# Sorted-block attention with a feed-forward stage: the first score blocks, a Sinkhorn row and the order of three transfers are rearranged

## The chip, the cores and the metric

The kernel runs on one core of a Trainium2 chip. A core has a matrix engine (TensorE; PE in the profile, PEld its weight loads), VectorE (DVE), ScalarE (ACT), GpSimd (POOL) and SyncE (SP), which here only issues transfers. The engines run their own instruction streams in order and wait for each other on semaphores. SP and POOL issue DMAs on one queue each; 16 DMA engines carry them. The metric is device time in microseconds (us) of the whole program, lower is better. The time before is 219.33 us, the median of three runs (218.88 to 220.26).

## The reference

Four batches of 8 heads, 768 tokens, 64 values a head. A learned 8 x 8 matrix a head is made doubly stochastic by five Sinkhorn rounds and then mixes the blocks of 96 keys and of 96 values; the queries attend within their block, and the result goes through a feed-forward layer with squared ReLU.

```python
P = sort_net
for _ in range(5):
    P = np.exp(P - np.max(P, axis=-1, keepdims=True))
    P = P / (np.sum(P, axis=-1, keepdims=True) + 1e-09)
    P = P / (np.sum(P, axis=-2, keepdims=True) + 1e-09)
k_sorted = np.einsum('bhij,bhjcd->bhicd', P, k_b)
v_sorted = np.einsum('bhij,bhjcd->bhicd', P, v_b)
scores = scale * np.matmul(q_b, k_sb.transpose(0, 1, 2, 4, 3))
attn = np.exp(scores - np.max(scores, axis=-1, keepdims=True))
attn = attn / (np.sum(attn, axis=-1, keepdims=True) + 1e-09)
x = np.matmul(attn, v_sb)                 # then (B*S, H*D) = (3072, 512)
g = s * np.maximum(x @ w_in, 0.0) ** 2 + b
return g @ w_out                          # w_in 512 x 2048, w_out 2048 x 512
```

## The kernel before, in words

The order of every engine's instructions is the order in which the program is written; nothing is rescheduled. So what follows is also the order of the queues.

**Tiles.** Each batch is worked in two halves of four blocks (384 tokens). PSUM is shared by two pools: `psa`, three buffers of two banks (tag a), and `psb`, two buffers of one bank (tag b). A matmul group that takes a buffer waits until the one that had it before has been read out. Key, value and query tiles (`KS`, `VS`, `QT`) stand in SBUF.

**Start.** SP loads the Sinkhorn matrix and batch 0's values (L77, L81). GpSimd issues all other loads: queries of half 0 (`qh`, L106), keys (L95), then the weights `wi` and `wo`, in an order that is fixed from the start. VectorE and ScalarE run the Sinkhorn rounds on the tile `sn`, 32 rows of 8 x 8 (L241 to L263). L248 is the exponential on ScalarE; between the rounds ScalarE also casts batch 0's values into `VP` (L206). The 1e-9 is added in the first round only, by an instruction of its own (L261) from a tile `eps`. Meanwhile TensorE multiplies zeros (`warm`, L132): 16 products of 256 columns, 102 of 80 columns with 64 weights, 6 of 512.

**Front** (L594 to L623). `spread_first` spreads batch 0's rows of `sn` over the partitions by a matmul with `emat` (L270) into `pe`. `build_pd` makes from it the mixing matrix `PD` on VectorE: product with a selector (L286), sum over j (L289), sum over that (L291), reciprocal (L293), scaled product (L295). `q_banks` transposes the queries of half 0 on TensorE, 48 transposes into two `psb` buffers, which VectorE and ScalarE copy out. `spread_later` spreads the rows of batches 1 to 3 into `pel`, copied by ScalarE (L282). Then `k_piece` and `k_banks` make the mixed keys, 16 columns a piece (64 or 2 x 16 matmuls), `v_piece` the mixed values, `s_banks` and `s_piece` the scores of a head pair with the exponential on ScalarE, `p_piece` the product with the values (L486), its reciprocal (L491) and scaling into `x` (L492), `t_piece` the transposes of `x` for the feed-forward layer (L503), and `part` its first products (L537). `evac` copies a PSUM tile on the engine named: D for VectorE, A for ScalarE. `v_piece` with `halves` copies its two halves apart, the second one when the function that it returns is called.

**The rest.** `ffn1(t)` (L537) and `ffn2(t)` (L563) are the feed-forward layer for half t, and carry the attention work of later batches in slots: slot i of `ffn1` behind product pair i, slot i of `ffn2` behind four products. For batches 2 and 3 the dictionary `s1` of `halves` places score pieces `SC(n, half, pair)` (L441), output pieces `P` and the transposing DMA `TD` of a finished half (`t_dma`, L512) into the slots of `ffn2(2b + 1)`. Values of batches 2 and 3 are mixed in `v_tiles`, written to DRAM by four DMAs (`v_back`, L415) and read back in another layout by two (L419, one for each z), and the queries are transposed by two DMAs (`q_dma`, L520), all four on SP's queue, in that order, from slot 2 of `ffn1(2b)`. `store` sends the result (L588, L591). `make_bias` waits for the scalar b and for the weights `wo`; behind its copies GpSimd issues the last three query loads of batch 1.

Of the kernel before, what the change touches and what calls it, by code (L numbers as in the profile page):

```python
# [22 lines left out]
def kernel(  # L23
# [51 lines left out]

    sn = const.tile([BH, NB, NB], FP)
    nc.sync.dma_start(out=sn, in_=sort_net.rearrange("b h i j -> (b h) i j"))  # L77
# [50 lines left out]

    def warm(n, w=512, m=128):
        z = psb.tile([128, 512], FP, tag="b", name="z")  # L130
        for _ in range(n):
            nc.tensor.matmul(out=z[0:m, 0:w], lhsT=zeros[:, 0:m], rhs=zeros[:, 0:w],  # L132
                             start=True, stop=True)
# [52 lines left out]
    rrec = const.tile([BH, NB], FP)  # L186
    eps = const.tile([BH, NB], FP)
    nc.vector.memset(eps, 1e-9)
    jsel = const.tile([128, NB], FP)
# [27 lines left out]

    def q_banks(b, half, engs):
        if b not in QT:
            QT[b] = trp.tile([128, 2, NHP, CQ, 64], BF, tag="qt", name="qt")  # L220
        pr = slice(half * 64, (half + 1) * 64)
        for u in range(2):
            tr = psb.tile([128, 1024], BF, tag="b", name="tqb")
            for a in range(2 * u, 2 * u + 2):
                for c in range(CQ):
                    for e in range(2):
                        o = (a % 2 * CQ + c) * 64
                        nc.tensor.transpose(out=tr[e * 64:(e + 1) * 64, o:o + 64],  # L228
                                            in_=QH[b][pr, 2 * a + e, c, :],
                                            identity=ident[pr, pr])  # L230
            evac(engs[u], QT[b][:, half, 2 * u:2 * u + 2].rearrange("p a c t -> p (a c t)"),
                 tr[:, 0:2 * TG])

# [9 lines left out]
                            op=ALU.subtract)  # L243
    warm(16, 256)
    warm(102, 80, 64)
    warm(6)
    for it in range(5):
        nc.scalar.activation(out=sn, in_=sn, func=AF.Exp)  # L248
        for c in {1: (0,), 3: (1,), 4: (2, 3)}.get(it, ()):
            permute(nc.scalar, 0, v0f, slice(c * CV, (c + 1) * CV))  # L250
        if it in (1, 2):
            idle[it - 1]()
        nc.vector.tensor_reduce(out=rstat, in_=sn, axis=AX.X, op=ALU.add)
        nc.vector.reciprocal(out=rrec, in_=rstat)
        nc.vector.tensor_tensor(out=sn, in0=sn, in1=rrec.broadcast_to([BH, NB, NB]), op=ALU.mult)
        if it == 4:
            break
        nc.vector.tensor_reduce(out=rstat, in_=sn.rearrange("p i j -> p j i"),
                                axis=AX.X, op=ALU.add)
        if it == 0:  # L260
            nc.vector.tensor_tensor(out=rstat, in0=rstat, in1=eps, op=ALU.add)  # L261
        nc.vector.reciprocal(out=rrec, in_=rstat)
        nc.vector.tensor_tensor(out=sn, in0=sn, in1=spread(rrec, [[0, NB], list(rrec.ap[1])]),  # L263
                                op=ALU.mult)
# [8 lines left out]
    def spread_first():  # L273
        pe = psb.tile([128, 512], FP, tag="b", name="pe")
        spread_rows(0, pe[:, 0:NB * NB])
        return pe[:, 0:NB * NB]

    def spread_later():
        ps = psa.tile([128, 2, 512], FP, tag="a", name="pel")
        for b in range(1, B):  # L280
            spread_rows(b, ps[:, 0, (b - 1) * NB * NB:b * NB * NB])
        nc.scalar.copy(out=later.rearrange("p b n -> p (b n)"), in_=ps[:, 0, 0:(B - 1) * NB * NB])  # L282

    def build_pd(b, rows):
        tmp = rtp.tile([128, NB, NB], FP, tag="tmp", name="tmp")
        nc.vector.tensor_tensor(out=tmp, in0=rows.rearrange("p (i j) -> p i j", j=NB),  # L286
                                in1=spread(jsel, [[0, NB], list(jsel.ap[1])]), op=ALU.mult)
        pt = rtp.tile([128, NB], FP, tag="pt", name="pt")
# [62 lines left out]

    def v_piece(b, d0, eng, halves=None):
        ps = psa.tile([128, CK, 2 * NG], FP, tag="a", name="tv")
        for d in range(CK):
            for z in range(2):
                nc.tensor.matmul(out=ps[z * GAP:(z + 1) * GAP, d, :],  # L356
                                 lhsT=VP[b % 2][:, d0 + d, :], rhs=PD[b][:, :, z, :],
                                 start=True, stop=True)
        if halves is None:
            evac(eng, VS[b % 2][:, :, d0:d0 + CK], ps[0:KR].rearrange("p d g -> p g d"))  # L360
            return None

# [4 lines left out]

        half(0, eng)
        return lambda eng: half(1, eng)

# [40 lines left out]
    def v_back(b):  # L411
        w = 2 * NC * D
        vd = drp.tile([2 * 2 * NB, NHP, 4, w], BF, tag="vd", name="vd")
        for c in range(4):
            nc.sync.dma_start(out=vd[:, :, c],  # L415
                              in_=RAW["v", b][c * 32:(c + 1) * 32].rearrange(
                                  "p (a x) d -> p a (x d)", a=NHP))
        for z in range(2):
            nc.sync.dma_start(  # L419
                out=VS[b % 2][z * GAP:z * GAP + C2, :, 0:D],  # L420
                in_=vd[z * 2 * NB:(z + 1) * 2 * NB].rearrange("i a c (y d) -> (c y) (i a) d", d=D))

# [238 lines left out]
    def VT(b, r): return lambda: v_tiles(b, r)  # L661
    def VB(b): return lambda: v_back(b)
    def TD(b, h): return lambda: t_dma(b, h)
    def PDB(b): return lambda: build_pd(b, later[:, b - 1, :])
    def QD(b): return lambda: q_dma(b)
    def LV(b): return lambda: load("v", b, 6, QT[b - 1][:, NB - 1, 0, 0:1])


    def halves(n):
# [4 lines left out]
        else:  # L674
            s0 = {0: [KP(n, 0), KP(n, 1), KP(n, 2)]}
        s1 = {0: [SC(n, 0, 0), SC(n, 0, 1)], 2: [SC(n, 0, 2), SC(n, 0, 3), SC(n, 1, 0)],
              3: [P(n, 0, 0)], 4: [P(n, 0, 1)], 5: [P(n, 0, 2)],
              6: [P(n, 0, 3), TD(n, 0), P(n, 1, 0)], 8: [SC(n, 1, 1), SC(n, 1, 2), SC(n, 1, 3)],
              9: [P(n, 1, 1)], 10: [P(n, 1, 2)], 11: [P(n, 1, 3), TD(n, 1)]}
        if n == 1:  # L680
            s1[0] = [VP2(n, 3, "AD")] + s1[0]
            s1[3] = s1.pop(2)
            s1[4] = [P(n, 0, 0)]
            s1[5] = [P(n, 0, 1), P(n, 0, 2)]
        if n + 1 < B:
# [22 lines left out]
    for b in range(1, B):  # L708
        n = b + 1
        s0, s1, u0, v0 = {}, {}, {}, {}  # L710
        if n < B:
# [4 lines left out]
            v0 = {0: [VT(n, 0)], 2: [VT(n, 1)]}  # L716
            u0 = {2: [VB(n), QD(n)]}
            if n + 1 < B:
# [35 lines left out]
```

## Time and profile before

| what | value |
|---|---|
| median of three runs | 219.33 us (218.88 to 220.26) |
| the profiled execution | 219.04 us, its span 217.3 us |
| VectorE, ScalarE, GpSimd busy | 125.4, 114.7, 71.9 us |
| feed-forward products, L537 and L563 | 86.7 and 81.7 us busy |
| first real matmul (L270) | 11.39 us |
| last matmul ends, last store lands | about 214.4, 216.3 us |
| TensorE's clock over the span | 0.992 of full speed |

The page gives busy times, a strip of 40 slices, the chain of work that ended last and the costliest groups of instructions. The chain names at each step who released it. "Idle before" is the time an engine stood still just before an instruction, with what ended it. A window's row gives the busy time of each engine in that stretch and the clock that TensorE was granted. All durations come from this one profiled execution.

### The profile page before, as it was taken

Reading aid. Unit: us, or ns where it says so; the run is one execution under the profiler, and the core shown is the slowest. Engines: PE = TensorE matmul, PEld = TensorE weight load, DVE = VectorE, ACT = ScalarE, POOL = GpSimd, SP = SyncE. Lnnn points to the kernel's source line nnn. Section 1 sums busy time; section 2 is a strip of 40 time slices with the busy share of each in tenths; the row PEclk is TensorE's granted clock in tenths of the full one; section 3 lists DMA queues with packets and bytes.
Section 4 is the critical chain, followed back from the end, with each engine's and each line's share of the span. In section 5 each row is a group of like instructions: output and inputs, shape, how many; then the busy total and the mean of one; then the engine's idle time right before and its main releaser. Section 6 shows DMA issues by size and latency. Waiting matters only on the chain.

```text
span 217.3 us, 5268 instructions
## 1 busy us (share of the span) xinstructions
PE 209.4 (96%) x2197; PEld 123.8 (57%) x2216; DVE 125.4 (58%) x259; ACT 114.7 (53%) x162; POOL 71.9 (33%) x129
## 2 busy tenths in 40 slices
PE   7999999999999999999999899999999999999994
PEld 5887666655455555565445556654445566654454
DVE  6767456558886986447537675448318644442122
ACT  4678687648986436565533447655341456650000
POOL 7659782789906025910050027610000000000000
PEclk9979999999999999999999999999999999999999
DMA  5999999999939948999989587999991550001212
GB/s 160 275 169 126 123 161 206 205 188 143 130 71 241 195 110 160 190 143 110 113 205 188 126 146 143 182 129 79 78 242 51 121 124 0 0 0 49 99 48 97
DMA packets 68023, 28.92 MB, mean 133 GB/s; under 512 B 51872, under 2 KB 64288, under 8 KB 68000
## 3 DMA queue, kind: packets, MB, share of 16 engines
q0 software_dynamic: 31168, 12.85, 52.9%
q1 hardware_dynamic: 36832, 15.74, 38.7%
q8 instruction: 17, 0.28, 0.6%
q14 instruction: 6, 0.05, 0.1%
HBM read 28.85 MB, written 7.86 MB: 169 GB/s over the span
## 4 chain that ended last, share of the span: by engine, by line
PE 73%; DMA 15%; DVE 5%; SPq 4%; issue 2%; ACT 1%; POOL 0%
PE ops L563 30%; PE hps L537 30%; DMA qt<-qtok 5%; DMA xt<-x 5%; DMA vd<-rawv 4%; PE pv L486 3%; SPq L419 3%; PE sc L441 2%; PE ops L580 2%; PE tv L356 1%; DVE x L492 1%; PE tp L315 1%; DMA sn<-in_sort_net_dram 1%; PE tqb L228 1%; PE tpp L328 1%
## 5 line engine op out<-in xcount | busy, mean ns | idle before, releaser
L537 PE MATMUL hps<-xt,wi 128*128 128x384 bf16 x512 | 86.7, 326 | 0.7 <-DMA xt<-x 0.5
L563 PE MATMUL ops<-wo,gt 128*128 128x512 bf16 x350 | 81.7, 379 | 1.9 <-issue 1.1
L551 ACT ACTIVATE rt<-hps 128x768 bf16<-128x768 f32 x64 | 51.8, 811 | 30.6 <-PE hps L537 29.4
L537 PEld LDWEIGHTS <-wi 128*128 128x128 bf16 x512 | 48.7, 98 | 33.2 <-issue 1.5
L552 DVE TENSOR_TENSOR gt<-rt 128x768 bf16<-128x768 bf16 x64 | 36.4, 571 | 40.4 <-ACT rt L551 40.3
L563 PEld LDWEIGHTS <-gt 128*128 128x128 bf16 x368 | 33.9, 98 | 36.7
L588 DVE SCALAR_TENSOR_TENSOR ot<-ops,s_bc,bias 128x512 f32<-128x512 f32 (+2 forms) x27 | 18.5, 690 | 30.6 <-PE ops L563 28.1
L449 ACT ACTIVATE at<-sc 112x768 bf16<-112x768 f32 x24 | 17.8, 808 | 26.8 <-PE sc L441 26.7
L492 DVE TENSOR_TENSOR x<-pv,rec 96x512 bf16<-96x512 f32 x32 | 22.0, 687 | 1.1
L117 POOL DMA_DIRECT2D qtok<-in_q_dram x24 | 18.6, 797 | 3.2 <-issue 1.7
L486 PEld LDWEIGHTS <-at 112*128 112x128 bf16 (+1 forms) x256 | 12.3, 101 | 5.6 <-ACT vs L214 0.3
L214 ACT CAST ks<-tpp 64x512 bf16<-64x512 f32 x18 | 13.1, 725 | 4.5 <-DVE ks L216 4.1
L142 POOL DMA_DIRECT2D wi<-in_moe_w_in_dram x24 | 12.9, 572 | 5.0 <-DMA rawk<-in_k_dram 3.1
L216 DVE CAST ks<-tpp 64x512 bf16<-64x512 f32 x18 | 13.1, 727 | 0.9 <-ACT ks L214 0.6
L486 PE MATMUL pv<-vs,at 112*128 112x66 bf16 (+1 forms) x256 | 12.9, 195 | 0.2 <-ACT vs L214 0.2
L95 POOL DMA_DIRECT2D rawk<-in_k_dram x21 | 11.2, 546 | 2.8 <-issue 1.8
L95 POOL DMA_DIRECT2D rawv<-in_v_dram x18 | 9.7, 555 | 5.4 <-DMA wo<-in_moe_w_out_dram 4.0
L132 PE MATMUL z<-zeros 128*64 128x80 bf16 (+2 forms) x123 | 9.6, 253 | 1.3 <-DVE zeros L120 1.2
L491 DVE RECIPROCAL rec<-pv 96x8 f32<-96x8 f32 x32 | 6.3, 198 | 5.5 <-PE pv L486 5.3
L132 PEld LDWEIGHTS <-zeros 128*64 128x64 bf16 (+1 forms) x124 | 7.3, 130 | 3.0 <-DVE zeros L120 1.2
L90 POOL COPY rawv<-qt 128x1 bf16<-128x1 bf16 x2 | 0.4, 189 | 23.4 <-DMA qt<-qtok 23.4
L408 ACT CAST rawv<-tvs 128x384 bf16<-128x384 f32 x4 | 1.9, 478 | 9.1 <-PE tvs L403 5.1
(101 smaller groups left out, 142.8 us busy)
## 6 DMA issues: line engine op xcount, KB each, us to landing
out_dram<-ot SPq DMA_DIRECT2D x22, 256.0 KB, 2.9
rawv<-in_v_dram POOLq DMA_DIRECT2D x18, 128.0 KB, 5.6
rawk<-in_k_dram POOLq DMA_DIRECT2D x18, 128.0 KB, 4.4
qtok<-in_q_dram POOLq DMA_DIRECT2D x24, 96.0 KB, 6.5
wo<-in_moe_w_out_dram POOLq DMA_DIRECT2D x4, 512.0 KB, 10.3
v0f<-in_v_dram SPq DMA_DIRECT2D x4, 384.0 KB, 5.3
vd<-rawv SPq DMA_DIRECT2D x8, 192.0 KB, 4.9
vs<-vd SPq DMA_DIRECT2D x4, 384.0 KB, 12.9
```

The source lines that it names most:

```text
L95: nc.gpsimd.dma_start(out=ti[:, c:c + n, :].rearrange("p c d -> p (c d)"), in_=raw["qkv".index(t)][b][:, c * D:(c + n) * D])
L117: nc.gpsimd.dma_start(out=QTOK[b][:, n], in_=qv[:, n])
L132: nc.tensor.matmul(out=z[0:m, 0:w], lhsT=zeros[:, 0:m], rhs=zeros[:, 0:w], start=True, stop=True)
L214: nc.scalar.copy(out=out, in_=in_)
L449: nc.scalar.activation(out=at, in_=sc[0:KR, :, 0:TG], func=AF.Exp, scale=scale)
L486: nc.tensor.matmul(out=pv[0:m, e, n * VW:(n + 1) * VW], lhsT=atf[:, c0:c0 + m], rhs=VS[b % 2][:, e * NG + g(n), :], start=True, stop=True)
L492: nc.vector.tensor_tensor(out=x[:, :, hp * 128:(hp + 1) * 128].rearrange("p n (e d) -> p e n d", e=2), in0=pvv[:, :, :, 0:D], in1=rec.unsq ...
L537: nc.tensor.matmul(out=H1[t, i][:, f, 0:TG], lhsT=wi[:, hp, fc:fc + 128], rhs=XT[t][:, :, hp, :], start=(hp == 0), stop=(hp == NHP - 1))
L551: nc.scalar.activation(out=rt, in_=h, func=AF.Relu)
L552: nc.vector.tensor_tensor(out=gt[:, 2 * i:2 * i + 2, :], in0=rt, in1=rt, op=ALU.mult)
L563: nc.tensor.matmul(out=ops, lhsT=gt[:, f, m * 128:(m + 1) * 128], rhs=wo[:, f, :], start=(f == 0), stop=(f == NF - 1))
L588: nc.vector.scalar_tensor_tensor(out=ot[:, ns], in0=ops, scalar=s_bc, in1=BIAS[0][:, ns], op0=ALU.mult, op1=ALU.add)
```

## The change

It has five parts.

1. Sinkhorn: `sn` becomes the first 8 rows of a tile `sne` with a ninth row set to 1e-9. The first round's sum over columns runs over the nine rows; the addition of `eps` goes. 
2. The zero products before the front become 42 of 256 columns; 8 more wait for a small memset (`gate`) that VectorE does in the fourth round. Three of 512 columns stand behind `spread_later`, in its tile's second bank.
3. `build_pd` takes the sum `cs` as the accumulated output of its first product (all batches); the reduction L291 goes.
4. Front: the transposes of the queries stand ahead of the first spread, their copies behind `build_pd`. `pe` takes a `psa` buffer. `later` is copied by VectorE. The first value piece stands ahead of `k_banks`, which is copied by ScalarE alone; two more value pieces stand ahead of the scores. The halves of the last two value pieces are copied by VectorE first, then by ScalarE.
5. Batches 2 and 3: SP issues read z = 0, query transpose 0, read z = 1, query transpose 1. In `ffn2(2b + 1)` three score pieces stand in slot 0 instead of two, the first output piece in slot 2 instead of 3, and the others follow a slot earlier, with the transposing DMA of half 0 in slot 5 instead of 6.

```diff
-    sn = const.tile([BH, NB, NB], FP)
+    sne = const.tile([BH, NB + 1, NB], FP)
+    sn = sne[:, 0:NB, :]
...
+    gate = const.tile([128, 16], BF)
+
+    def warm(n, w=512, z=None, behind=None):
+        if z is None:
+            z = psb.tile([128, 512], FP, tag="b", name="z")
+        if behind is not None:
+            nc.tensor.matmul(out=z[:, 0:16], lhsT=zeros[:, 0:128], rhs=behind,
+                             start=True, stop=True)
...
-    eps = const.tile([BH, NB], FP)
-    nc.vector.memset(eps, 1e-9)
+    nc.vector.memset(sne[:, NB:NB + 1, :], 1e-9)
...
-    warm(16, 256)
-    warm(102, 80, 64)
-    warm(6)
+    warm(42, 256)
     for it in range(5):
...
+        if it == 3:
+            nc.vector.memset(gate, 0.0)
+            warm(8, 256, behind=gate)
...
-        nc.vector.tensor_reduce(out=rstat, in_=sn.rearrange("p i j -> p j i"),
+        nc.vector.tensor_reduce(out=rstat, in_=(sn if it else sne).rearrange("p i j -> p j i"),
                                 axis=AX.X, op=ALU.add)
-        if it == 0:
-            nc.vector.tensor_tensor(out=rstat, in0=rstat, in1=eps, op=ALU.add)
...
     def spread_later():
         ps = psa.tile([128, 2, 512], FP, tag="a", name="pel")
         for b in range(1, B):
             spread_rows(b, ps[:, 0, (b - 1) * NB * NB:b * NB * NB])
-        nc.scalar.copy(out=later.rearrange("p b n -> p (b n)"), in_=ps[:, 0, 0:(B - 1) * NB * NB])
+        warm(3, z=ps[:, 1])
+        nc.vector.tensor_copy(out=later.rearrange("p b n -> p (b n)"), in_=ps[:, 0, 0:(B - 1) * NB * NB])
...
-        nc.vector.tensor_tensor(out=tmp, in0=rows.rearrange("p (i j) -> p i j", j=NB),
-                                in1=spread(jsel, [[0, NB], list(jsel.ap[1])]), op=ALU.mult)
+        cs = rtp.tile([128, 1], FP, tag="cs", name="cs")
+        nc.vector.scalar_tensor_tensor(
+            out=tmp, in0=rows.rearrange("p (i j) -> p i j", j=NB), scalar=1.0,
+            in1=spread(jsel, [[0, NB], list(jsel.ap[1])]), op0=ALU.mult, op1=ALU.mult, accum_out=cs)
         pt = rtp.tile([128, NB], FP, tag="pt", name="pt")
         nc.vector.tensor_reduce(out=pt, in_=tmp, axis=AX.X, op=ALU.add)
-        cs = rtp.tile([128, 1], FP, tag="cs", name="cs")
-        nc.vector.tensor_reduce(out=cs, in_=pt, axis=AX.X, op=ALU.add)
...
-    def q_dma(b):
+    def q_dma(b, vd=None):
         ti = QTOK.pop(b)
         qt = trp.tile([128, NB, NHP, BLK], BF, tag="qt", name="qt")
         for n0 in (0, HB):
+            if vd is not None:
+                v_read(b, vd, n0 // HB)
             nc.sync.dma_start_transpose(
...
+    qe = q_banks(0, 0)
     build_pd(0, spread_first())
-    q_banks(0, 0, "DA")
+    qe("DA")
     spread_later()
     k_piece(0, 0, "D")
     k_piece(0, CK, "A")
-    k_banks(0, 2 * CK, "DA")
     v_piece(0, 0, "D")
+    k_banks(0, 2 * CK, "AA")
+    v_piece(0, CK, "D")
+    v2 = v_piece(0, 2 * CK)
     s_banks(0, 0, 0)
     s_piece(0, 0, 1)
-    v_piece(0, CK, "D")
-    v2 = v_piece(0, 2 * CK, "A", 1)
-    v3 = v_piece(0, 3 * CK, "A", 1)
-    v2("D")
+    v2(0, "D")
+    v3 = v_piece(0, 3 * CK)
+    v3(0, "D")
+    v2(1, "A")
+    v3(1, "A")
     s_banks(0, 0, 2)
-    p_piece(0, 0, 0, 3)
-    v3("A")
+    p_piece(0, 0, 0)
     p_piece(0, 0, 1)
...
-        s1 = {0: [SC(n, 0, 0), SC(n, 0, 1)], 2: [SC(n, 0, 2), SC(n, 0, 3), SC(n, 1, 0)],
-              3: [P(n, 0, 0)], 4: [P(n, 0, 1)], 5: [P(n, 0, 2)],
-              6: [P(n, 0, 3), TD(n, 0), P(n, 1, 0)], 8: [SC(n, 1, 1), SC(n, 1, 2), SC(n, 1, 3)],
+        s1 = {8: [SC(n, 1, 1), SC(n, 1, 2), SC(n, 1, 3)],
               9: [P(n, 1, 1)], 10: [P(n, 1, 2)], 11: [P(n, 1, 3), TD(n, 1)]}
...
+            s1.update({0: [SC(n, 0, 0), SC(n, 0, 1), SC(n, 0, 2)],
+                       2: [SC(n, 0, 3), P(n, 0, 0), SC(n, 1, 0)], 3: [P(n, 0, 1)],
+                       4: [P(n, 0, 2)], 5: [P(n, 0, 3), TD(n, 0)], 6: [P(n, 1, 0)]})
```

`v_read(b, vd, z)` is the read of L419 for one z. Batch 1 keeps its slots.

More of the change, by code (lines that the diff above doesn't have):

```diff
@@ L127 @@
     nc.scalar.activation(out=dummy, in_=zeros[:, 0:1], func=AF.Exp)
-    def warm(n, w=512, m=128):
-        z = psb.tile([128, 512], FP, tag="b", name="z")
+    gate = const.tile([128, 16], BF)
[5 more added lines that the diff above has]
+                             start=True, stop=True)
         for _ in range(n):
-            nc.tensor.matmul(out=z[0:m, 0:w], lhsT=zeros[:, 0:m], rhs=zeros[:, 0:w],
+            nc.tensor.matmul(out=z[:, 0:w], lhsT=zeros[:, 0:128], rhs=zeros[:, 0:w],
                              start=True, stop=True)
@@ L216, in evac, with q_banks @@
             nc.vector.tensor_copy(out=out, in_=in_)
-    def q_banks(b, half, engs):
+    def q_banks(b, half, engs=None):
         if b not in QT:
@@ L221, in q_banks @@
         pr = slice(half * 64, (half + 1) * 64)
+        trs = []
         for u in range(2):
             tr = psb.tile([128, 1024], BF, tag="b", name="tqb")
+            trs.append(tr)
             for a in range(2 * u, 2 * u + 2):
@@ L230, in q_banks, with move @@
                                             identity=ident[pr, pr])
-            evac(engs[u], QT[b][:, half, 2 * u:2 * u + 2].rearrange("p a c t -> p (a c t)"),
-                 tr[:, 0:2 * TG])
+        def move(engs):
+            for u in range(2):
+                evac(engs[u], QT[b][:, half, 2 * u:2 * u + 2].rearrange("p a c t -> p (a c t)"),
+                     trs[u][:, 0:2 * TG])
+        if engs is None:
+            return move
+        move(engs)
     idle = [
@@ L273, in spread_first @@
     def spread_first():
-        pe = psb.tile([128, 512], FP, tag="b", name="pe")
-        spread_rows(0, pe[:, 0:NB * NB])
-        return pe[:, 0:NB * NB]
+        pe = psa.tile([128, 2, 512], FP, tag="a", name="pe")
+        spread_rows(0, pe[:, 0, 0:NB * NB])
+        return pe[:, 0, 0:NB * NB]
     def spread_later():
@@ L350, in k_banks, with v_piece @@
             evac(eng, KS[b % 2][:, :, :, c1:c1 + CK // 2], ps.rearrange("p c z g -> p g z c"))
-    def v_piece(b, d0, eng, halves=None):
+    def v_piece(b, d0, eng=None):
         ps = psa.tile([128, CK, 2 * NG], FP, tag="a", name="tv")
@@ L358, in v_piece @@
                                  start=True, stop=True)
-        if halves is None:
+        if eng is not None:
             evac(eng, VS[b % 2][:, :, d0:d0 + CK], ps[0:KR].rearrange("p d g -> p g d"))
-            return None
         def half(h, eng):
@@ L366, in half @@
                  ps[0:KR].rearrange("p d (g i) -> p g i d", i=NB)[:, :, hs])
-        half(0, eng)
-        return lambda eng: half(1, eng)
+        return half
     def v_pairs(b, d0, engs):
@@ L417, in v_back, with v_read @@
                                   "p (a x) d -> p a (x d)", a=NHP))
[L418 to L421, printed above, removed]
+        return vd
+    def v_read(b, vd, z):
+        nc.sync.dma_start(
+            out=VS[b % 2][z * GAP:z * GAP + C2, :, 0:D],
+            in_=vd[z * 2 * NB:(z + 1) * 2 * NB].rearrange("i a c (y d) -> (c y) (i a) d",
+                                                          d=D))
     AT = {}
@@ L661, in VT, with QD @@
     def VT(b, r): return lambda: v_tiles(b, r)
-    def VB(b): return lambda: v_back(b)
     def TD(b, h): return lambda: t_dma(b, h)
     def PDB(b): return lambda: build_pd(b, later[:, b - 1, :])
-    def QD(b): return lambda: q_dma(b)
+    def QD(b): return lambda: q_dma(b, v_back(b))
     def LV(b): return lambda: load("v", b, 6, QT[b - 1][:, NB - 1, 0, 0:1])
@@ L675, in halves @@
             s0 = {0: [KP(n, 0), KP(n, 1), KP(n, 2)]}
-        s1 = {0: [SC(n, 0, 0), SC(n, 0, 1)], 2: [SC(n, 0, 2), SC(n, 0, 3), SC(n, 1, 0)],
-              3: [P(n, 0, 0)], 4: [P(n, 0, 1)], 5: [P(n, 0, 2)],
-              6: [P(n, 0, 3), TD(n, 0), P(n, 1, 0)], 8: [SC(n, 1, 1), SC(n, 1, 2), SC(n, 1, 3)],
+        s1 = {8: [SC(n, 1, 1), SC(n, 1, 2), SC(n, 1, 3)],
               9: [P(n, 1, 1)], 10: [P(n, 1, 2)], 11: [P(n, 1, 3), TD(n, 1)]}
         if n == 1:
[L681 to L684, printed above, removed]
+            s1.update({0: [VP2(n, 3, "AD"), SC(n, 0, 0), SC(n, 0, 1)],
+                       3: [SC(n, 0, 2), SC(n, 0, 3), SC(n, 1, 0)], 4: [P(n, 0, 0)],
+                       5: [P(n, 0, 1), P(n, 0, 2)], 6: [P(n, 0, 3), TD(n, 0), P(n, 1, 0)]})
+        else:
+            s1.update({0: [SC(n, 0, 0), SC(n, 0, 1), SC(n, 0, 2)],
+                       2: [SC(n, 0, 3), P(n, 0, 0), SC(n, 1, 0)], 3: [P(n, 0, 1)],
+                       4: [P(n, 0, 2)], 5: [P(n, 0, 3), TD(n, 0)], 6: [P(n, 1, 0)]})
         if n + 1 < B:
@@ L716 @@
             v0 = {0: [VT(n, 0)], 2: [VT(n, 1)]}
-            u0 = {2: [VB(n), QD(n)]}
+            u0 = {2: [QD(n)]}
             if n + 1 < B:
```

## The prediction

> **What bounds the kernel now.** First the page: how much is TensorE idle at all?
>
> ```profile
> PE 209.4 (96%) x2197; PEld 123.8 (57%) x2216; DVE 125.4 (58%) x259; ACT 114.7 (53%) x162; POOL 71.9 (33%) x129
> ...
> PEclk9979999999999999999999999999999999999999
> ```
>
> TensorE is busy 209.4 of 217.3 us, and the third slice has a granted clock of 0.7. So the kernel is bound by TensorE, and a change gains only by starting the real matmuls sooner, by removing holes, or by removing that dip. The profiled execution took 219.04 us (span 217.3, and 1.7 around it), 0.29 below the median 219.33; I add and subtract from 219.04. Next the chain of waits, in order of time (start, length, what):
>
> ```profile
> 11.03 0.23 DVE sn L255
> 11.25 0.14 issue
> 11.39 0.40 PE pe L270 x2
> 11.79 0.88 PE tqb L228 x48
> 12.67 0.81 PE pel L270 x6
> 13.48 1.82 PE tp L315 x64
> 15.30 0.85 PE tkb L346 x32
> 16.15 0.87 PE tv L356 x32
> 17.04 1.24 DVE vs L216
> ```
>
> Until 11.25 the chain is the Sinkhorn loop on VectorE (the busy TensorE there does filler products). From 11.39 it is TensorE in program order: 48 query transposes stand between the first spread and the key tiles. Then the granted clock, in four stretches of 3.41 us (start:end, length, then busy us and instructions of PE, PEld, DVE, ACT, POOL, then clock, DMA share, GB/s):
>
> ```profile
> 10.08:13.49 3.41, 2.87 (x64) 2.12 (x64) 2.29 (x10) 3.29 (x5) 0.88 (x2) 1.00 1.16 202
> 13.49:16.90 3.41, 3.41 (x128) 3.38 (x128) 1.98 (x3) 2.25 (x4) 2.85 (x6) 0.50 1.10 137
> 16.90:20.31 3.41, 3.16 (x127) 2.56 (x123) 2.99 (x3) 2.81 (x6) 3.41 (x7) 1.00 1.06 128
> 20.31:23.73 3.42, 3.07 (x54) 2.40 (x54) 2.86 (x9) 2.93 (x7) 2.73 (x6) 1.00 1.09 131
> ```
>
> The clock is halved for exactly one stretch, 13.49 to 16.90, right behind the stretch with the least work on PE. Last, PE's waits from 100 us on (who, for whom, us in total, times, longest):
>
> ```profile
> PE hps L537 <- DMA xt<-x: 0.5, 1, 0.5
> PE sc L441 <- DMA qt<-qtok: 0.2, 1, 0.2
> ```
>
> These two are the only waits on data there, at 124.5 (batch 2, first half's transposed output) and 158.9 (batch 3, query transposes). Everything else after 26 us is TensorE back to back.
>
> **The change, part by part.**
>
> *Sinkhorn.* The 1e-9 add (L261) goes: 0.19 us, from its start at 4.31 to the next at 4.50. The ninth row makes one reduction 72 elements long instead of 64; two reductions of 64 take 0.21 and 0.26, so at most 0.03 more. The memset of that row replaces the memset of `eps`; the `gate` memset (that of `eps` took 0.07) falls into VectorE's 0.32 us wait for Exp. If that cover were gone it would cost 0.07. `sn` is ready at 11.06 instead of 11.24, and the first spread starts at 11.20 instead of 11.39.
>
> *Query transposes first.* They wait for `qh`, which by the trace lands at 9.62, and take 0.8 to 0.9 us: 9.75 to 10.6, done 0.6 before the spread. Their cover is the Sinkhorn loop. If `qh` landed later than 10.3 they would hold up the spread one for one. Both fillers before them are over: 42 products of 256 columns at 0.213 (their spacing up to 6.6 us) and 0.109 behind that end near 8.4; the 8 behind `gate` run from about 8.45 to 9.4.
>
> *Behind the spread.* TensorE then has 6 spread products (0.13 apart, as at 12.60 to 13.21), 0.79, and three 512-column fillers at 0.216 (spacing of the fillers at 10.04 to 10.47), 0.65: 11.46 to 12.9. VectorE: tmp, pt, rc, pd at their old spacings 0.26, 0.25, 0.20, 0.35 from 11.64, the L291 sum (0.20) gone: pd ready at 12.70, plus 0.12 to reach PE. No row has a product with an accumulated sum; between the plain product tmp (0.22) and the larger L295 (0.35), plus a second instruction as long as the sum removed, pd comes at 12.70 to 13.0. I take 12.8; the fillers hide it. So `tp` starts at 12.9 instead of 13.41: 0.5 us.
> The Trainium skill ("VectorE: DVE Perf Modes", Two Vector instructions with no wait between them) says that an operation that writes out its accumulator is two instructions, the operation and an accumulator read. By it pd would come at the 13.0 end and the sum would be 0.1 smaller; no run here shows it yet.
>
> *Order of the tiles.* With the clock at full, a 32-product group takes 0.5 us (value tiles from 17.38) against 0.85 in the halved stretch. VectorE then evacuates without a hole: tp0 at 13.6, value tiles at 14.8 and 15.9 (starts 1.14 apart, as 17.04 and 18.19), two halves at 17.0 and 17.9. Before, its fourth value evacuation ended at 20.37; now at 18.6. VectorE got the copy of `later` (0.30) and lost a key evacuation (0.69); ScalarE got the second small key evacuation (0.59) and lost the copy. ScalarE: tp1 14.1 to 15.1, two `tkb` to 16.15, three Exps 16.6 to 18.25, two value halves to 19.3. `pv` of the first head pair needs `v2`'s buffer, freed at 18.8: it starts at 18.9 instead of 20.31. But ScalarE's Exps of the third score tile end at 20.1 (before: 21.02), the fourth's scores wait for them, and the last x ends at 23.0 instead of 24.22. The next transposes of queries start at 24.9 instead of 26.0: **1.0 us**, of which 0.7 is the dip that is not there (the same replay of the old order at full clock ends 0.7 earlier) and 0.35 the order itself.
>
> *Does the dip go?* The stretch ahead of it had 2.87 us of PE, 0.95 of it transposes, so 1.92 of other products. The new order puts into the same stretch two and six spreads (0.40 and 0.88 in busy time), the three fillers (about 0.8) and 0.5 of key tiles: about 2.5 without transposes. The stretch from 20.31 held full clock with 3.07, of which three groups of output transposes (0.33 each) are 1.0: 2.1 of others. 2.5 is above it, 1.92 below; so in the same alignment the dip goes. (With transposes counted, 2.87 lost the clock, 3.07 held it, and the new order has about 3.0: less clear.)
> The Trainium skill ("TensorE: Matmul & The Clock Gate", Part 1, and Part 4 on transposes) has a free-running window of 3413 ns and says that transposes do not count as busy in the same way. The length agrees with the trace (3.41); by a free-running window the alignment changes from run to run.
>
> *Batches 2 and 3.* `v_read` of half 0, transposes of query half 0, then `v_read` and transposes of half 1, instead of both reads first. On SP's queue the first transpose is moved past one read: before, SP issued the second read for 5.84 us and the transpose landed at 158.98; now one read less is ahead, and it lands some 6 us earlier. The 0.26 hole at 158.9 closes (0.2 and the semaphore). The third scores move to slot 0, the first output piece to slot 2, and the transposing DMA of half 0 to slot 5, one slot (4 products, 0.87) earlier; the wait at 124.5 (0.5) closes, since its landing at 124.86 moves by more than that. The stores queued behind it on SP have DMA landings of 2.9 us and no one on PE waits for them. Scores 0 to 2 fill all three `psa` buffers; the first Exp (0.81) frees one long before the 8 products (1.73) to slot 2 are over, so no new wait. Sum: **0.7**.
>
> Last, `make_bias`: VectorE waits for `b_bc` there anyway (1.6), and the query loads behind it set when batch 1's second transpose lands (65.8). Its scores start at 67.1, so at most 1.2 us of the front's gain gets past this point; 1.0 does. Total 219.04 - 1.0 - 0.7 = 217.3; with the accumulator's upper end 217.4.
>
> **Rivals.**
>
> *A: the clock drops all the same.* With the 3.41 us stretches set 0.7 to 1.9 earlier against the program, one would lie between the `gate` fillers' end (9.4) and `tp` (12.9), where only the spreads and part of the fillers count: 1.3 to 1.7 us, below the 1.92 that lost the clock. Key and value tiles then run at 0.85 per group. If it drops over 13.49 to 16.90 as before, replaying gives 25.97 for the next transposes: no gain in the front, 219.04 - 0.7 = 218.3; a drop from 11.5 on gives 26.5, 218.9. Against it: the sum above. For it: the hole behind 9.4 is new, and the runs before differ by 1.4 us (218.88 to 220.26), as a dip that wanders would make them.
> By the free-running window of the Trainium skill ("TensorE: Matmul & The Clock Gate", Part 1) this case comes and goes from run to run; the one trace here cannot show that.
>
> *B: slower: the second half's value read and query transposes come late.* They are now queued behind the first transpose. Two reads in flight together took 16 us (141.15 to 157.2), so one alone takes 8; the transpose lands about 3 us behind the read before it. If each waits for the landing of the one before, batch 3 has 141.15 + 8 + 3 + 8 + 3 = 163.2 against 160.2, where its scores are due in slot 2, and batch 2 has 92.2 + 22 = 114.2 against 112.5: 4.7 us in all, 222.0. With the reads' own 12.9 each it would be 23 us, 241. It decides from a landing after 160.2 on. For it: SP needed 8.5 us to issue the first transpose behind the reads, until 156.1, one us before the second read had landed. Against it: by that row SP goes on one us before the landing, and the bytes are the same; so the end comes near 160 as before (second issue at 156.7 and 3.9 to land, 160.6).
>
> *C: the mid gain is lost.* As B, but late by only 0.5 to 1 us at batch 3: with the front's gain and that at batch 2, 217.9 to 218.5.
>
> *D: `qh` late or other waits I do not see in the front*: a loss of 0.5 there, 218.0 to 219.5.
>
> **How the numbers follow.** Forecast 217.4 with 0.46 (own range 216.8 to 217.9: 0.1 for the accumulator, 0.2 for the hole at 158.9, 0.3 for the profiled run against the median). A 0.25 (218.3), C and D together 0.16, B 0.08, and 0.05 for more gain than counted, below 216.8. Range 216.8 to 219.0: it takes in A, C and most of D, and leaves B and the last case out. A difference of 1% is 2.2 us, 217.1 or 221.5 against the median; that is about what a measurement can tell. Faster: the 0.05 and four tenths of the forecast, 0.23. Slower: B, 0.08. Same: 0.69.
>
> **What would show it.** Right: `tp` starting near 12.9, granted clock 1.00 from 13.5 to 17, the first `pv` at 18.9, query transposes of half 1 near 24.9, no PE wait on xt<-x or qt<-qtok after 100 us. Wrong: a halved stretch between 11 and 17 (A), PE waits on qt<-qtok in slot 2 of batch 2 or 3 (B, C), the spread waiting for transposes (D), or pd later than 13.0.

## The result, and the profile after

The changed kernel takes 221.5 us (median of six runs, 220.53 to 223.25) against 218.8 before: ratio 1.0123 [1.0087, 1.0159], slower by 2.7 us. The forecast was 217.4, with a range of 216.8 to 219.0. The profiled execution took 223.06 us, its span is 221.0.

The page's row of TensorE and its clock strip:

```profile
PE 208.4 (94%) x2124; PEld 122.2 (55%) x2143; DVE 124.3 (56%) x260; ACT 114.7 (52%) x161; POOL 71.3 (32%) x129
PEclk9999699999999999999999999999999999999999
```

TensorE is busy 208.4 us, 1.0 less than before, in a span that is 3.7 longer: it stands still more. The dip of the clock has moved from the third slice to the fifth. The chain of waits (start, length, what) shows where it stands:

```profile
11.16 0.40 PE pe L284 x2
11.56 0.67 PE pel L284 x6
12.23 0.16 issue
12.39 0.59 PE pel L139 x2
12.98 1.13 PE tp L330 x64
14.12 0.51 PE tv L371 x32
14.62 0.25 PE tkb L361 x16
14.88 2.38 issue
17.25 0.44 PE tkb L361 x16
...
20.59 0.49 ACT vs L220
21.07 0.18 issue
21.25 0.38 PE scb L475 x8
```

Down to 14.62 everything comes as forecast. Then TensorE stops between the 16th and the 17th of 32 like products, whose tile it already has and whose operands landed at 13.44 at the latest, for 2.4 us in which the profile shows nothing that it waits for. The windows (start:end, length, then busy us and instructions of PE, PEld, DVE, ACT, POOL, then clock, DMA share, GB/s):

```profile
13.49:16.90 3.41, 1.39 (x88) 1.30 (x83) 2.36 (x2) 1.82 (x3) 2.65 (x5) 1.00 1.27 163
...
23.56:26.97 3.41, 3.41 (x28) 2.32 (x26) 1.81 (x5) 1.62 (x4) 2.05 (x5) 0.50 0.87 88
```

The old dip at 13.49 is not there, but TensorE does only 1.39 us of work in that stretch. From 23.56 the granted clock is halved for 3.41 us (a dip), while the first feed-forward products run. The waits of the whole (who, for whom, us in total, times, longest):

```profile
PE tkb L361 <- issue: 2.4, 1, 2.4
PE hps L555 <- DMA xt<-x: 1.3, 1, 1.3
...
PE scb L475 <- ACT vs L220: 1.0, 1, 1.0
```

The wait for xt<-x is at 79.7, in batch 1. The two waits behind 100 us that the forecast wanted closed are closed. So the query transposes of half 1 start at 28.54 instead of 26.00, batch 1's first scores at 66.03 instead of 63.48, and batch 1's own first half at 81.02 instead of 77.02: 2.5 lost in the front, 1.4 at xt, and about 0.3 won back behind.

**What stands at 14.68.** The trace also records the transfers that carry instructions: 17 packets of 16384 bytes on a queue of their own. Count TensorE's recorded instructions in order of time: a weight load and a product are two, and the few semaphore waits of its sequencer are counted too. A hole is the time from the start of one instruction to the start of the next. These are the first two such packets and the instruction that starts late:

```
kernel          packet          last before it, next      hole   next minus packet's end
before          11.10 to 12.07  no. 448: 14.47, 14.52     0.04
before          15.25 to 16.21  no. 705: 17.79, 17.81     0.03
after           14.84 to 15.78  no. 448: 14.68, 17.25     2.57   1.47
after           18.52 to 19.88  no. 704: 20.14, 21.25     1.11   1.38
```

There are two holes, 256 instructions apart. The page puts the second one down to ScalarE's copy of `vs`; but the score products there take the two `psb` buffers of the first scores, and the Exps that read those out had ended at 19.51 and 19.89, before the hole. Theory F: TensorE runs out of its block of 256 instructions and waits for the next. The block behind no. 448 would be asked for when no. 192 is reached. Before, that was at 8.4, among 124 zero products, which are 248 instructions; the change makes 51 of them, and no. 192 falls into the query transposes at 10.44. The packet starts 4.4 us later. Rival G: the key product or its buffer is late. Rival H: the new order of the tiles is slow by itself.

### The profile page after: what moved, and what is told of

Its sections match the earlier page's. It is cut to its first block, busy times and chain, and to the rows that moved or that the text cites. A ratio compares the mean times of both kernels' runs of the same rounds, so it can differ in the third digit from the quotient of the medians.

```text
span 221.0 us, 5123 instructions
## 1 busy us (share of the span) xinstructions
PE 208.4 (94%) x2124; PEld 122.2 (55%) x2143; DVE 124.3 (56%) x260; ACT 114.7 (52%) x161; POOL 71.3 (32%) x129
## 4 chain that ended last, share of the span: by engine, by line
PE 86%; DVE 4%; DMA 3%; issue 3%; ACT 2%
PE hps L555 39%; PE ops L581 33%; PE pv L502 3%; DMA xt<-x 3%; PE sc L457 2%; PE ops L598 2%; PE tpp L343 1%; ACT at L480 1%; PE scb L475 1%; DVE x L508 1%; PE tr L519 1%; PE tv L371 1%; DMA sne<-in_sort_net_dram 1%; DVE sne L271 1%; ACT sne L261 1%
## 5 line engine op out<-in xcount | busy, mean ns | idle before, releaser
L555 PE MATMUL hps<-xt,wi 128*128 128x384 bf16 x512 | 87.6, 329 | 1.3 <-DMA xt<-x 1.3
L570 DVE TENSOR_TENSOR gt<-rt 128x768 bf16<-128x768 bf16 x64 | 35.7, 559 | 42.5 <-ACT rt L569 42.3
L606 DVE SCALAR_TENSOR_TENSOR ot<-ops,s_bc,bias 128x512 f32<-128x512 f32 (+2 forms) x27 | 18.6, 691 | 26.9 <-PE ops L581 23.5
L118 POOL DMA_DIRECT2D qtok<-in_q_dram x24 | 18.6, 801 | 1.7 <-issue 1.3
L502 PE MATMUL pv<-vs,at 112*128 112x66 bf16 (+1 forms) x256 | 13.5, 197 | 0.0
L139 PE MATMUL z<-zeros 128*128 128x256 bf16 x50 | 8.2, 345 | 1.2 <-DVE zeros L121 1.2
L139 PEld LDWEIGHTS <-zeros 128*128 128x128 bf16 x53 | 6.3, 123 | 3.2 <-DVE zeros L121 1.2
```

Of the source, the lines that this page charges most:

```text
L118: nc.gpsimd.dma_start(out=QTOK[b][:, n], in_=qv[:, n])
L139: nc.tensor.matmul(out=z[:, 0:w], lhsT=zeros[:, 0:128], rhs=zeros[:, 0:w], start=True, stop=True)
L502: nc.tensor.matmul(out=pv[0:m, e, n * VW:(n + 1) * VW], lhsT=atf[:, c0:c0 + m], rhs=VS[b % 2][:, e * NG + g(n), :], start=True, stop=True)
L555: nc.tensor.matmul(out=H1[t, i][:, f, 0:TG], lhsT=wi[:, hp, fc:fc + 128], rhs=XT[t][:, :, hp, :], start=(hp == 0), stop=(hp == NHP - 1))
L570: nc.vector.tensor_tensor(out=gt[:, 2 * i:2 * i + 2, :], in0=rt, in1=rt, op=ALU.mult)
L606: nc.vector.scalar_tensor_tensor(out=ot[:, ns], in0=ops, scalar=s_bc, in1=BIAS[0][:, ns], op0=ALU.mult, op1=ALU.add)
```

## The experiments

Each set has its own runs of the kernel before, with medians of 219.33, 219.16, 219.15, 219.44 and 219.12 us. "Full clock" is a run with a mean granted clock of 0.995 or more; one dip of 3.41 us makes 0.992, two make 0.984.

**Sixteen instructions fewer ahead of it (e2).**

```diff
-    warm(42, 256)
+    warm(34, 316)
```

> The changed kernel with 34 zero products of 316 columns in place of 42 of 256: the same time for TensorE, 16 instructions fewer. Theory F: the hole moves by 16 instructions, from the 17th of the 32 tkb products to the 25th, and again lies right behind the 448th instruction of the trace; 1.5 to 2.6 us long. Theory G: it stays at the 17th product.

One run, 223.09 us. TensorE's timeline (start, us, what, idle before):

```profile
14.46 0.55 PE L361 MATMUL tkb<-pd,rawk 128*64 128x64 bf16 x24
16.84 0.32 PE L361 MATMUL tkb<-pd,rawk 128*64 128x64 bf16 x8 [1.84 <-issue]
```

The hole has moved from behind the 16th product to behind the 24th, and is again behind instruction 449, 1.29 us after its packet ended. G falls: it goes by the number of the instruction.

**The kernel before with as few zero products (e3, e6).**

```diff
-    warm(16, 256)
-    warm(102, 80, 64)
+    warm(43, 256)
```

That is e3; e6 has `warm(43, 306)` there.

> The kernel before with 49 zero products (43 of 256 columns and the 6 of 512) in place of 124, same time for TensorE; nothing else. Theory F: instruction 448 now falls into the first value group (tv), near 16.3 us, and the fetch of its block is asked for only in the query transposes near 12.4: a hole of 0.5 to 2 us there that the kernel before does not have, time 219.3 to 221. Theory G and H: fillers are only fillers, the time stays at 218.7 (218.3 to 219.1) and no hole comes.

221.32 us, 1.0097 [1.006, 1.0133]. This edit also changed the time: the fillers ended at 9.2, TensorE idled 2.1 us, and the clock was halved from 11.7 to 18.6. With TensorE slow, the first block came in time; behind no. 705 there was a hole of 1.0. As the clock alone could explain the time, it was repeated with longer products:

> The kernel before with 49 zero products, the first 43 of 306 columns so that they last as long as its 118 (in run e3 they ended 1.7 us early, and the clock fell for 6.8 us). Theory F: block changes fall behind instructions 448 (first value group, near 16) and 704 (scores, near 19); the fetch for the first is asked for only at 12.4. A hole of 0.5 to 2 us at one of the two, behind exactly that instruction, and 219.3 to 221 us. If instruction blocks do not matter: no hole, 218.5 to 219.3.

220.83 us, 1.0092 [1.0056, 1.0128], in the profiled execution at full clock, and 220.3 to 221.0 in the six runs at full clock. The profiled execution's waits:

```profile
PE tv L355 <- issue: 2.1, 1, 2.1
...
PE scb L458 <- issue: 0.9, 1, 0.9
```

Both holes are there, behind instructions 449 (2.30 us) and 705 (1.10), each ending 1.4 us after its packet. The kernel before, with nothing but fewer and longer zero products, loses 2.0 us. So H is not needed for the main loss, and neither is the clock.

**The changed kernel with as many zero products as before (e1, e5).**

```diff
-    warm(42, 256)
+    warm(115, 104)
```

That is e5; e1 has `warm(16, 256)` and 99 products of 64 columns with 64 weights there.

> The changed kernel with 124 zero products ahead of the front, as many as before, in place of 51 (16 of 256 columns and 99 of 64 in place of 42 of 256); nothing behind them differs. Theory F: the hole of 2.6 us in the key tiles at 14.7 is TensorE waiting for its next 16384-byte block of instructions; blocks change every 256 instructions, here behind 192, 448, 704 of those in the trace. With 73 more products (146 instructions) the 192nd is passed near 7 us instead of 10.4, its fetch starts before 12, the 448th falls into the first key piece (tp) and finds its block there: no hole of more than 0.5 us between 13 and 16, granted clock 1.00 up to 24, query transposes of half 1 near 25 instead of 28.5, time 217.5 to 219. Theory G: the hole belongs to the key product or its buffer (a key load or a copy that comes late): it stays at the 17th product of tkb with 2.4 us, time 221 to 222. Theory H: the new order of tiles is slower by itself (ScalarE has both small key copies), whatever the fetch: time above 220 with no hole in tkb.

220.59 us, 1.0065 [1.0034, 1.0097]. No hole in the key tiles, 0.43 behind no. 705. But that is above 220 without the hole, the sign that H had been given. Seven of twelve runs had two dips or three (median 220.7), and the three at full clock have a median of 219.2; in the profiled execution, with three dips, the queries landed 1.2 us late for TensorE as well. So, with products of the full width:

> The changed kernel with 115 zero products of 104 columns and full weights in place of 42 of 256, about as many columns and so about as long (run e1 had narrow ones and lost the clock). Theory F (late block of instructions): instruction 448 lies in the first key piece and its block is there; no hole over 0.5 us in tkb, granted clock 1.00 up to 24, query transposes of half 1 at 25.0 to 25.5, as the prediction had them (24.9). How much of that reaches the end: if the front's gain passes (the prediction's step, floor 1.2 us away), 217.4 to 217.8; if batch 1 stands on its loads (theory L: VectorE waits for the scalar b, and the key loads land, at fixed times near 48 to 53), the front's gain is lost between 45 and 64 and only the 0.6 of the middle remains, 218.3 to 218.8. Theory G (the key product itself): hole in tkb, 221 to 222.

220.48 us, 1.0049 [1.0018, 1.008]. The time expected, 218.8 at most, was not reached. The hole behind no. 448 is gone; the one behind no. 704 is 1.06. In the profiled execution, at full clock, the front's longest waits are

```profile
PE tqb L236 <- DMA qh<-in_q_dram: 0.9, 1, 0.9
PE tv L371 <- issue: 0.9, 1, 0.9
```

and the query transposes of half 1 come at 26.22; without the hole that would be 25.2, an estimate. More than half the loss is back, and two things are left: the second block, and two dips in five of twelve runs.

**Another place for the blocks (e9), and the change once more (e12).**

```diff
-    warm(42, 256)
+    warm(95, 126)
```

> The changed kernel with 95 zero products of 126 columns (104 with the 9 behind gate and before it; 51 in the change, 124 in run e5). By theory F instruction 448 now lies near the end of the first key piece and 704 some 370 instructions behind tp's first, where the third and fourth value pieces wait for buffers anyway; the request for the first block is made near 8, for the second near 13.9. Expected: holes without a wait of at most 0.5 us in all between 13 and 19 (e5 had 0.9), 219.4 to 220.3. If the position did not matter beyond e5's: a hole of 1 us again and 220.5; if the new order of the tiles is what costs: no hole and still 220.5.

Median 220.49 us, ratio 1.0027 [0.9992, 1.0063]. The hole behind no. 705 fell to 0.39, but in an execution whose first key tiles ran at half clock (12.26 to 15.68), so the place is not shown to be better. The median is what the expectation had for "the new order is what costs". The runs are mostly of two kinds: 218.4 to 219.2 in four at full clock (a fifth took 221.1), 220.5 to 221.0 in six with two dips.

> The changed kernel once more, on the chip of these runs. Theory F: the hole lies behind instruction 448 again, in the key tiles, though its length may be another (1.5 to 2.6 us), and the time is 220.8 to 222. If the hole came from something that comes and goes: no hole there, or another place.

221.62 us, 1.0121 [1.0076, 1.0167], and all seven runs have two dips. In this execution the first key tiles ran in a halved stretch:

```profile
13.27:16.68 3.41, 3.41 (x119) 3.17 (x118) 2.18 (x4) 1.68 (x2) 2.44 (x5) 0.50 1.15 149
```

TensorE reached no. 448 only at 16.47 and found its block. There is no hole there, contrary to what F expected, one of 1.37 us behind no. 705, and a second dip from 23.51. So the first hole comes and goes, but in a way that fits F: a slow TensorE arrives after the block, a fast one before it. Either way the front is late; the query transposes of half 1 come at 28.21 here and at 28.54 in the first profile.

**Why the packet is late (e11).**

```diff
     k_piece(0, 0, "D")
+    nc.gpsimd.tensor_copy(out=scr0, in_=KS[0][:, 0, 0, 0:1])
+    for c in range(4):
+        if c == 3:
+            load_qh(0, 1, 4)
+        for a in range(NHP):
+            load_wi(c * W8, (c + 1) * W8, slice(a, a + 1))
...
```

The block of loads and memsets from the first `wi` load to batch 1's first query loads is moved here.

> The changed kernel with all weight loads, and what GpSimd issues behind them, held back until the first key piece is copied out (a GpSimd copy of one column that reads it). Theory F1 (the fetch is late because it queues among the data transfers): the 16384-byte packet, asked for at 10.4, starts once the key loads are through, by 13.2 instead of 14.8, and the hole behind instruction 448 is under 1.2 us instead of 2.4. Theory F2 (the fetch has its own delay, or is asked for only when the block runs out): the packet starts at 14.6 to 15 and the hole is 2 us or more. The whole takes longer either way, 222 to 227, since the weights come some 3 us later.

One run, 224.46 us. The packet started at 13.04, with the last packets of the key loads, instead of 14.84, as F1 (the fetch queues among the data transfers) had it. But that is 2.0 us behind no. 192, and with the weight loads in flight the other profiles have 2.0 to 3.1 there, the changed kernel's first one alone 4.4. So why that packet was so late stays open. TensorE had a halved clock here and reached no. 448 at 15.83, after the block, so a shorter hole was not seen.

**The clock (e13, e14, e16).** In e9, TensorE's windows:

```profile
19.09:22.50 3.41, 2.09 (x50) 1.63 (x44) 2.48 (x7) 3.02 (x8) 3.41 (x8) 1.00 1.08 143
22.50:25.92 3.42, 3.37 (x27) 2.41 (x27) 1.68 (x4) 1.61 (x4) 3.06 (x6) 0.50 0.86 87
```

It waits for ScalarE's Exps and a copy of VectorE in the first (0.6 us each), and the clock falls in the second. Theory C is that the little work in the first brings the dip. Zero products there (e13), and more of them between 9 and 11 too (e14):

```diff
-    p_piece(0, 0, 0)
-    p_piece(0, 0, 1)
+    p_piece(0, 0, 0, 3)
+    p_piece(0, 0, 1, 4)
...
-    p_piece(0, 0, 2)
+    p_piece(0, 0, 2, 3)
```

> Run e9 with 3, 4 and 3 zero products of 240 columns ahead of the first three output pieces (the change had taken out the 3 of the kernel before). In e9 TensorE was busy 2.09 of the 3.41 us from 19.09, and the clock fell for the 3.41 us behind it. Theory C: about 1.0 us more work there, as much as the kernel before has (3.05), so the second dip goes: no run at 0.984, the runs with one dip near 0.992 at 219 to 219.8, the median 218.9 to 219.8. If the lack of work is not what drops the clock: half of the runs again at 0.984 with 220.7, median 220.5.

219.55 us, 1.0022 [0.9994, 1.0049]. No run had two dips, five had one. The same stretch in its profile, at full clock behind it:

```profile
19.46:22.87 3.41, 2.86 (x53) 2.52 (x53) 2.22 (x5) 3.02 (x7) 3.23 (x7) 1.00 1.13 147
```

```diff
-    warm(42, 256)
+    warm(86, 139)
...
-            warm(8, 256, behind=gate)
+            warm(13, 256, behind=gate)
...
+        warm(4, 256, z=pe[:, 1])
         spread_rows(0, pe[:, 0, 0:NB * NB])
```

This is what e14 has besides (e13 has e9's 95 products at the start).

> Run e13 with five more zero products behind gate and four ahead of the first spread (nine fewer at the start, so that block changes stay where they are). Theory C: both dips go, clock 1.00 in nearly all runs, 218.4 to 219.0. If only the second depends on products: as e13.

219.81 us, 1.0004 [0.9978, 1.003]. Nine of twelve at full clock, three with one dip. The clock is held, and within the interval nothing of the loss is left; but the hole behind no. 705 was 1.84 us in its profile (1.21 in e15's), at the same place in the program as in e9 and now at full clock, and the time expected was not reached.

```diff
-    p_piece(0, 0, 0, 3)
+    p_piece(0, 0, 0)
```

e16, the kernel before:

> The kernel before without the three zero products ahead of its first output piece. Theory C: with 0.3 us less work in the stretch from 20.3 the clock falls behind it in some runs, a third or more of them below 0.995 (3 to 5 of 30 before), and the median is 219.2 to 220. If these products do nothing: 219.1 and at most 2 of 12 below 0.995.

219.4 us, 1.0 [0.9976, 1.0025], all twelve at full clock. So it is not those three products as such, and C as it stands is wrong for the old order, which does without them. As far as e13 and e14 go, it is the waits of the new order, which zero products can cover; to that extent H, the order being slow by itself, was right. How much work keeps the clock stays open. In the changed kernel's first profile the stretches of 3.41 us, counted back from the dip at 23.56, have 1.55 us of work from 13.32 and 2.03 from 20.15: full clock follows the first, the dip the second.

**The middle alone (e4), and with the two small parts of the front (e10).**

```diff
-            u0 = {2: [VB(n), QD(n)]}
+            u0 = {2: [QD(n)]}
```

and the rest of part 5 as in the change, in the kernel before:

> The kernel before with the fifth part alone (order of the value reads and query transposes on SP's queue, scores and output pieces of batches 2 and 3 a slot earlier). If the prediction's sum for this part holds: the waits at 124.5 and 158.9 go, 0.7 less, 218.0 against 218.7. If the transposes come late (rival B): waits on qt<-qtok and a time above 219. If nothing is gained because something else is late there: 218.7.

218.82 us, 0.9973 [0.995, 0.9995]: 0.6 us faster, of 0.7 forecast, and no wait of TensorE behind 100 us.

e10 has parts 1 and 3 besides:

```diff
-        nc.vector.tensor_reduce(out=cs, in_=pt, axis=AX.X, op=ALU.add)
...
-        if it == 0:
-            nc.vector.tensor_tensor(out=rstat, in0=rstat, in1=eps, op=ALU.add)
```

> Parts 1, 3 and 5 of the change without 2 and 4: ninth row, accumulated sum and the middle, with the fillers and the order of the front as before. Theory F with theory L: instruction counts are those of the kernel before, so no new hole; the 0.3 to 0.4 us that parts 1 and 3 bring in the front do not pass batch 1: 218.6 to 218.9, like part 5 alone (218.8). If the front's gain passes: 218.3 to 218.5. If one of parts 1 and 3 costs: above 219.2.

218.93 us, 0.998 [0.9953, 1.0008]: as expected from part 5 alone. But its profile has a hole of 0.81 behind no. 705, which the expectation had ruled out. So have other profiles of the old order with its 124 zero products: 0.40 in e4, 0.85 in e16, 1.02 in e17, all at full clock. In e8, also at full clock, and in the kernel before, with its key tiles at half clock, there is none. The second hole is not the change's alone.

**Does a gain of the front pass batch 1 (e7, e8, e15, e17)?** Theory L is that batch 1 stands on its loads. The loads of `s_bc` and `b_bc` go ahead of those of `wo`, in e5 (e7), the kernel before (e8), e14 (e15) and e10 (e17).

```diff
+    for t, src in ((s_bc, moe_s), (b_bc, moe_b)):
+        nc.gpsimd.dma_start(out=t, in_=src.to_broadcast([128, 1]))
     for c in range(4):
         fs = slice(c * (NF // 4), (c + 1) * (NF // 4))
...
-    for t, src in ((s_bc, moe_s), (b_bc, moe_b)):
-        nc.gpsimd.dma_start(out=t, in_=src.to_broadcast([128, 1]))
```

> Run e5 with the loads of the two scalars s and b issued ahead of the wo loads. Theory L: VectorE no longer waits for b at 48, the front's gain gets further, 0.3 to 1.0 us less than e5 (217.5 to 218.2); the rest of it is lost at the key loads of batch 1, which land at 51 to 53. If the scalar does not matter: as e5 within 0.2.

> The kernel before with the two scalars loaded ahead of wo. TensorE waits for nothing there in its profile, so by theory L it gains 0 to 0.3 us (219.0 to 219.3 against 219.3); a gain of 0.5 or more would say that the kernel before stood on this wait already.

> Run e14 with the two scalars loaded ahead of wo. Theory L: with the clock held and the holes small, the front arrives at batch 1 some 0.5 us or more earlier than with e4, and what stops it there is the scalar b: 0.2 to 0.6 less than e14, 218.0 to 218.6. If it stands on the key loads: as e14 within 0.2.

> Run e10 (parts 1, 3 and 5, old front) with the two scalars loaded ahead of wo. Theory L: VectorE's wait of 2.2 us for b goes, and 0.3 to 0.5 us more of the front's gain arrives at batch 1's scores: 218.2 to 218.7 beside before at 219.2. If batch 1 stands on its key loads, which move back by as much as the scalars move forward: as e10, ratio 0.998 within 0.002.

e7: 220.49 us, 1.004 [1.001, 1.007], nothing beyond e5; e8: 219.24, 0.9993 [0.9961, 1.0024]; e15: 219.56, 1.0006 [0.9978, 1.0033]; e17: 218.86, 0.9972 [0.9939, 1.0004], beside 0.998 without the edit. In the times it does nothing that can be told from none. One profile of each suggests what happens (when things start, us):

```
                                   before    e4     e10    e17
query transposes of half 1          26.00   25.10  25.34  25.52
second layer of batch 0's half 0    50.09   48.98  49.23  49.62
batch 1's first scores              63.48   64.09  62.94  63.01
```

In e4 the clock held and the front came 1.1 us earlier to the second layer, and batch 1's scores 0.6 later: VectorE waited 3.3 us for b (1.6 before) and the last keys landed at 53.5 (51.4 before). e10 kept 0.5 of 0.9; e17, without that wait, all 0.5 that it had.

## Why the prediction was wrong, and where it was right

- **Right, to 0.1 us:** the Sinkhorn part (spread at 11.16, forecast 11.20), the transposes hidden before it (9.76 to 10.70), `tp` at 12.91 (12.9). In e12 the queries landed at 10.72 and the spread came at 11.64, so the first half of rival D, late `qh`, is real in some executions.
- **Right, and cheaper than its bounds:** the accumulated sum.

```profile
L302 DVE SCALAR_TENSOR_TENSOR tmp<-pe,jsel x1: 225/225/225, 11.6 to 11.6; 128x64 f32<-128x64 f32 x1
L302 DVE DVE_READ_ACCUMULATOR tmp<-pe,jsel x1: 84/84/84, 11.7 to 11.7; 128x1 f32 x1
```

The read takes 84 ns (min, median and max of one), and from `tmp` to `pt` it is 0.27 us instead of 0.26; the sum of 0.20 that it replaces is gone. `pd` starts at 12.19 and is ready at 12.54, ahead of the 12.70 to 13.0 of the forecast, so it was the zero products that held `tp` until 12.91. That it is an instruction of its own is what the Trainium skill had said ("VectorE: DVE Perf Modes", Two Vector instructions with no wait between them).
- **Failed, and the largest: the order of the tiles** ("`pv` at 18.9", "query transposes at 24.9"). They came at 21.53 and 28.54. The replay had waits on data, buffers and engines, and took the zero products by their time alone, as filler; it never counted instructions. Replacing 124 of them by 51 moved every later block change by some 140 instructions, and the new order at full clock uses up its blocks faster than they come: from no. 448 (17.25) it is 1.27 us to the start of the next packet, 1.35 to its end and 1.38 until TensorE goes on, 4.0 in all, where `tp`, two value groups and a key group are 320 instructions and, by the prediction's own 1.0 and 0.5 a group, 2.5 us. This is the second half of rival D, "other waits I do not see", which was priced at 0.5. In e12's profile a halved stretch took the place of the first hole. Nor does any profile show the 0.35 that the order itself was to bring: with the second hole subtracted (an estimate), the query transposes come at 25.2, 24.8 and 26.0 in e5, e14 and e15, and with the old order at 24.5 to 25.7 in e4, e8, e10, e16 and e17.
The Trainium skill has the rule ("Runtime: NRT & Kernel Launch", Instruction fetch mechanics): instructions come in blocks of 16 KiB, 256 each, by the sequencer's own transfers, while the current block runs; it calls the cost mostly hidden. Size and spacing agree with the trace (16384 bytes, holes behind 448 and 704); hidden it is in the kernel before (0.03 and 0.04 us), and not in the changed one (2.57 and 1.11).
- **Failed: "0.7 is the dip that is not there".** Of the 142 runs of the kernel before beside the experiments, 122 are at full clock. The one profile that I had showed an exception. In the front the dip was real: five profiles of the old order at full clock (e4, e8, e10, e16, e17) have the query transposes at 25.10 to 25.74 instead of 26.00. But the 20 runs with a dip have a median of 219.3 against 219.2 for the others, so no cost at the end is to be seen, and its removal could bring little. Of the changed kernel's 13 runs twelve have a dip and ten of them two. Where they lie only two profiles tell: at 23.56 in the first, at 13.27, as rival A had it, and 23.51 in e12.
- **Wrong readings on the way.** The stretch from 20.31 holds two groups of output transposes (0.67 us), not three, so its other work is 2.4 us, not 2.1, and the 2.5 of the new order is hardly above it. In rival B, reads of 12.9 each make 24.3 us and 241.6, not 23 and 241, which changes nothing.
- **Failed: "at most 1.2 us of the front's gain gets past this point; 1.0 does".** The point named was the second query transpose; e4's profile shows the loads of b and of the keys closing earlier. Only single profiles show this; in the times it was not resolved.
- **Right in size: the middle,** 0.7 forecast, 0.6 [0.1, 1.1] measured (e4). Rival B did not come: a value read takes 7.4 us (median) instead of 12.9, and SP goes on before it has landed.

## What to carry to other kernels

Filler products have a number as well as a length: a change of their count shifts every later block of instructions, so where small products run densely beside heavy loads, count instructions as well as time. Moving the block change with more fillers took the first hole away (e5); no place was found here that closes the second at full clock. A dip or a wait seen in one profile is worth removing only if the other runs have it and if the next stage isn't standing on a transfer anyway. Part 5 alone (e4) is the one version that is faster than the kernel before clear of the interval, by 0.3%; the whole change is not.

## What the runs showed of the hardware

- In twenty holes of 0.28 to 2.57 us over 17 profiles, TensorE went on 1.24 to 1.47 us after the end of the 16384-byte packet (once 1.69), always behind instruction 448 or 449, or 704 or 705. The packet took 0.9 to 1.4 us, and started 0.3 to 4.4 us after the instruction 256 ahead of that place had begun. In three of them (the second ones of the change, e2 and e12) the page names a copy of ScalarE as what ended the wait; in e2 the product that starts late does need such a copy, so part of that hole may be a wait for it.
- The same packets may hold up transposing transfers, but this is a likeness over profiles and not shown. Batch 1's first xt<-x took 5.2 to 6.4 us in the six profiles with 43 to 51 zero products at the start, where a packet starts 2.7 to 3.6 us behind its issue, and 3.9 to 4.3 in eleven of the other thirteen (4.9 and 5.3 in two). But of all 27 such transfers with a packet at that distance, in any batch, twelve took 5.2 to 6.4 us and fifteen 3.8 to 4.0. So what made the 1.3 us at 79.7 stays open; it belongs to the loss, and comes in 0.4 to 1.7 us in all six of those profiles.
